# Retention attention and a feed-forward layer in one kernel: second-half queries get a state of their own from unit 6 on, and two of the three attention visits move

## The chip, the cores and the metric

The kernel runs on one core of one Trainium2 chip. The metric is the device time of one execution in microseconds (us). PE is TensorE's matmul side, PEld its weight loads, DVE is VectorE, ACT is ScalarE, POOL is GpSimd, SP is SyncE, which issues most of the DMAs.

## The reference, cut to what matters

Inputs are `q`, `k`, `v` of shape 4 x 8 x 768 x 64 (batch, head, time, width), `w_in` 512 x 2048, `w_out` 2048 x 512 and one `alpha` for each of the 2048 hidden columns.

```python
gamma = 1.0 - 2.0 ** (-5.0 - np.arange(H))
for t in range(S):
    state = gamma * state + k[:, :, t] (outer) v[:, :, t]
    y[:, :, t] = scale * q[:, :, t] @ state
x = y as (B*S, H*D)
h = x @ w_in
out = (np.maximum(h, 0.0) + alpha * np.minimum(h, 0.0)) @ w_out
```

The attention is linear with a decay per head, so it can be done in chunks: inside a chunk by masked scores (q times k, mask, times v), from earlier chunks by a 64 x 64 state per head.

## The kernel before

Time is cut into 12 units of 256 steps, three for each batch element, and each unit into two chunks of 128 (`c` = 0, 1). Two units make a block of 512 rows for the feed-forward layer: six blocks, n = 0 to 5. In each of the later blocks the kernel runs the first matmul stage of block n (`ffn1`: 16 groups of four 128x512 matmuls, L450, each followed by a RELU copy on ACT, L461, and a DVE operation, L463), then the second (`ffn2_seven`), and inside the second it does the attention of the two units of the next block, `u0 = 2 * (n + 1)` and `u0 + 1`.

`ffn2_seven` forms the 512 x 512 result from seven products of 16 matmuls (128x256, L536) instead of eight. They run on two PSUM banks, `ox` (bank 0) and `oy` (bank 1):

- product 1 into `ox`, copied to SBUF by ACT (`kept`, L552, tile `cu`)
- product 2 into a fresh `oy`; DVE adds the copy and stores it (`plus`, L557, tile `os`)
- product 3 added onto `ox`, copied by `kept` (L552)
- product 4 into a fresh `oy`
- product 5 added onto `ox`, using the sum `gs(2)`; copied by `kept` (L552); `plus` (L557) adds `oy` to it
- product 6 added onto `ox`, copied by ACT (L598)
- product 7 added onto `oy`, using `gs(3)`; `plus` (L557)

The sums `gs` of the activations are DVE operations (`g_sums`, L434). The order on every engine is the program's own: `tick(gen, m)` issues the next m matmuls of the products and whatever follows them, and between ticks the attention work is written by hand.

The attention work of a block, as it is before the change, comes in three visits of PE:

- after 8 ticks: `sum_mm` (L249) of both units, the state contribution k times v of each chunk, as 64x64 matmuls, and `score_mm` (L315) of `u0`, two halves of the heads in banks (4, 5) and (6, 7)
- after 48 ticks: `out_mm` of `u0` (state part L364, masked part L382), with its two evictions on ACT (`take_y`, L405, tile `xT`), and `score_mm` of `u0 + 1`
- after 80 ticks: `out_mm` of `u0 + 1` and its evictions

The 256 steps of a unit are kept so that a chunk's 128 keys come as two halves of 64 (`r` = 0, 1). A second-half key touches only second-half queries, so the scores and the masked part use 128 columns for `r` = 0 and 64 for `r` = 1.

The running state goes through `state_sum` and `state_copy`. `state_sum` (L274, L275): DVE adds the contribution in PSUM to the state so far (`ss`), POOL multiplies by the decay (`tf`); the next chunk starts from that. `state_copy` turns `tf` into f16 operands for `out_mm` (tile `th` from unit 6 on): one 64-row half on POOL (L301, `part` 0), the other on ACT (L299, `part` 1). `masks` (L328) are DVE multiplications from PSUM to f16, four for each unit, 384 elements wide.

POOL prepares the next units in `rescale` (L176) and `cast_v` (L192). The first `rescale` of a block waits for `gate`, the last `g_sums` of the block before. SP then transposes (`turn_dma`, L196) and moves the queries (`move_q`, L204); stores and loads share SP's queue. `tab` holds the decay (`dec`), `mj` the mask, `ps(bank, name)` names one of eight PSUM banks.

Of the kernel before, what the change touches and what calls it, by code (L numbers as in the profile page):

```python
# [9 lines left out]
FP = mybir.dt.float32  # L10
F16 = mybir.dt.float16
COPY = mybir.ActivationFunctionType.Copy
SUB = mybir.AluOpType.subtract
RELU = mybir.ActivationFunctionType.Relu
MULT = mybir.AluOpType.mult
ADD = mybir.AluOpType.add
# [5 lines left out]
def kernel(  # L22
# [10 lines left out]
    nc = tc.nc  # L33
# [3 lines left out]
    NP = H // 2  # L37

    SPLIT = 4

    FLIP = 6
    U = 256
    UPB = S // U
# [3 lines left out]
    scale = 1.0 / np.sqrt(D)  # L51
# [9 lines left out]
    for h in range(H):  # L61
        for r in range(2):
            j = 2 * (p_ar % 64) + r
# [10 lines left out]
    sbp = ctx.enter_context(tc.tile_pool(name="sbp", bufs=1, space=bass.MemoryType.SB))  # L74
# [7 lines left out]
    mj = sbp.tile([128, 512], F16, tag="mj", name="mj")[:, 0:384]  # L82
    dec = tab[:, OD : OD + NP].unsqueeze(2).to_broadcast([128, NP, 64])
# [10 lines left out]
    def ps(bank, name, dt=FP, n=512):  # L94
        return psp.tile([128, n], dt, tag=f"b{bank}", name=name)
# [8 lines left out]
    tgbuf = [sbp.tile([128, NP, 128], F16, tag=f"tg{i}", name=f"tg{i}") for i in range(6)]  # L104

    staged, prepped, live, tgs, xT, gts, gsums = {}, {}, {}, {}, {}, {}, {}
    moved = {}
    held, late = [], []

    def behind(ins, other):  # L110
# [20 lines left out]
    def rows(x):  # L131
        return slice(64 * x, 64 * x + 64)

    def load(u, parts="kqv"):
        if u >= NU:
            return
        b, c = divmod(u, UPB)
        t = staged.setdefault(u, {})
        for nm in parts:
            src = {"k": k, "q": q, "v": v}[nm[0]]  # L140
            if nm[0] not in t:
                t[nm[0]] = sbp.tile(
                    [128, H, 2 * D], FP, tag=f"{nm[0]}s", bufs=3, name=f"{nm[0]}s{u}"
                )
            h = slice(0, H) if len(nm) == 1 else slice(4 * int(nm[1]), 4 * int(nm[1]) + 4)
            if u >= SPLIT and nm != "q":
                for x in range(2):
                    for y in range(2):
                        at = U * c + 128 * x + 64 * y
                        nc.sync.dma_start(  # L150
                            out=t[nm][rows(x), :, D * y : D * y + D],
                            in_=src[b, :, at : at + 64, :].rearrange("h p d -> p h d"),
                        )
                continue
            hold(
                nc.sync.dma_start(
                    out=t[nm[0]][:, h, :],
                    in_=src[b, h, U * c : U * c + U, :].rearrange(
                        "h (p r) d -> p h (r d)", r=2
                    ),  # L160
                )
            )
# [70 lines left out]
    def qmove(kq, a, c, p):  # L233
        return kq.rearrange("p (t r a) i -> p t r a i", t=2, r=2)[rows(a), 1, :, p, rows(c)]
# [3 lines left out]
    def sum_mm(u, banks, half=0):  # L238
# [17 lines left out]
        for c in cs:  # L256
            sums[u, c] = sums["t"][c][:, 256 * half : 256 * half + 256].rearrange(
                "p (a e) -> p a e", e=64
            )

    def state(u, c, eng, copy="gg"):

        state_copy(state_sum(u, c, eng), copy)

    def state_sum(u, c, eng):
        if (u, c) not in sums:
            return None
        s = sums.pop((u, c))
        t = sbp.tile([128, NP, 64], FP, tag="tf", bufs=4, name=f"tf{u}_{c}")
        if u % UPB == 0 and c == 0:  # L270
            nc.vector.tensor_tensor(out=t, in0=s, in1=dec, op=MULT)
        else:
            ss = sbp.tile([128, NP, 64], FP, tag="ss", bufs=3, name=f"ss{u}_{c}")
            nc.vector.tensor_tensor(out=ss, in0=run.pop(), in1=s, op=ADD)  # L274
            eng.tensor_tensor(out=t, in0=ss, in1=dec, op=MULT)  # L275
        run[:] = [t]
        return u, c, t

    def state_copy(uct, copy="gg", part=None):

        if uct is None:
            return
        u, c, t = uct
        to = (u, 1) if c == 0 else (u + 1, 0)
        if to[0] >= FLIP:
            tg = tgs.get(to) or tgs.get((to[0], 1 - to[1]))
            if tg is None:
                tg = sbp.tile([128, 2, NP, 64], F16, tag="th", bufs=3, name=f"th{to[0]}")
        else:
            tg = tgbuf[(2 * u + c) % len(tgbuf)]  # L290
        tgs[to] = tg
        for a in range(2):
            far = to[0] >= FLIP and a != to[1]
            if part is not None and far != part:
                continue
            i = t[rows(a)]
            o = tg[rows(to[1]), a] if to[0] >= FLIP else tg[rows(a), :, rows(a)]
            if far or copy[a] == "a":
                nc.scalar.activation(out=o, in_=i, func=COPY, bias=0.0, scale=1.0)  # L299
            else:  # L300
                nc.gpsimd.tensor_copy(out=o, in_=i)  # L301
# [92 lines left out]
    def take_y(u, cs, eng=None):  # L394
        n, ul = divmod(u, 2)
        if n not in xT:
            xT[n] = sbp.tile([128, 2, NP, U], F16, tag="xT", bufs=2, name=f"xT{n}")
        ys = live[u]
        for c in cs:
            o = xT[n][:, ul, :, 128 * c : 128 * c + 128].rearrange("k a (p r) -> k a r p", r=2)  # L400
            i = ys[c].rearrange("k (a r p) -> k a r p", r=2, p=64)
            if eng is not None:
                eng.tensor_copy(out=o, in_=i)
                continue
            nc.scalar.activation(  # L405
                out=o,
                in_=i,
                func=COPY,
                bias=0.0,
                scale=1.0,  # L410
            )
# [11 lines left out]
    def g_sums(n, i, lo, hi):  # L423

        if n not in gsums:
            gsums[n] = sbp.tile([128, 4, HF, U], F16, tag="gt", bufs=2, name=f"gs{n}")
        g = gts[n].rearrange("p (k f) (j t) -> p k f j t", k=2, j=2)
        a11, a12 = g[:, 0, lo:hi, 0, :], g[:, 1, lo:hi, 0, :]
        a21, a22 = g[:, 0, lo:hi, 1, :], g[:, 1, lo:hi, 1, :]
        s1, s2, s3, s4 = (gsums[n][:, x, lo:hi, :] for x in range(4))  # L430
        o, a, b, op = (
            (s1, a21, a22, ADD), (s2, s1, a11, SUB), (s3, a11, a21, SUB), (s4, a12, s2, SUB)
        )[i]
        return nc.vector.tensor_tensor(out=o, in0=a, in1=b, op=op)  # L434
# [177 lines left out]
    def tick(gen, m=10**6):  # L612
        for _ in range(m):
            if next(gen, 1) == 1:
                return
# [171 lines left out]
    for n in range(1, NBLK):  # L787
        more = n + 1 < NBLK
        u0 = 2 * (n + 1)
        if n > 1:  # L790
            gen = ffn1(n, (7, 2, 3, 1, 0, 6, 5, 4, 7, 1, 0, 4, 5, 6, 7, 1))
            if more:
                for u in (u0, u0 + 1):
                    i = rescale(G, u, 0, 0, 8)
                    if u == u0:
                        behind(i, gate)
                    rescale(G, u, 1, 0, 8)
                    turn_dma(u)
                    cast_v(G, u)
                    if u > u0:  # L800
                        load(u + 1, "qv")
                    else:
                        load(u + 2, "k")
                    move_q(u)
                    tick(gen, 8)
            tick(gen)
        gen = ffn2_seven(n, 0, 1) if more else ffn2_seven(n, (0, 3), 1, 2)
        if more:
            tick(gen, 8)
            sum_mm(u0, (2, 3))  # L810
            sum_mm(u0 + 1, (2, 3), half=1)
            score_mm(u0, 0, (4, 5))
            score_mm(u0, 1, (6, 7))
            s00 = state_sum(u0, 0, G)
            state_copy(s00, part=0)
            masks(u0, 0)
            s01 = state_sum(u0, 1, G)
            masks(u0, 1, (0,))
            masks(u0, 1, (1,))
            s10 = state_sum(u0 + 1, 0, G)  # L820
            tick(gen, 8)
            state_copy(s00, part=1)
            state_copy(s01, "aa")
            state_copy(s10, part=0)
            tick(gen, 17)
            state_copy(s10, part=1)
            load(u0 + 3)
            s11 = state_sum(u0 + 1, 1, G)
            state_copy(s11, part=0)
            g_sums(n, 2, 0, HF)  # L830
            tick(gen, 15)
            out_mm(u0, (4, 5))
            score_mm(u0 + 1, 0, (6, 7))
            score_mm(u0 + 1, 1, (2, 3))
            state_copy(s11, part=1)
            masks(u0 + 1, 0)
            masks(u0 + 1, 1)
            gate = g_sums(n, 3, 0, HF)
            tick(gen, 32)
            out_mm(u0 + 1, (4, 5))  # L840
        else:
            tick(gen, 33)
            g_sums(n, 2, 0, HF)
            g_sums(n, 3, 0, HF)
        tick(gen)
# [30 lines left out]
```

## Time and profile before

| what | value |
|---|---|
| median of three runs | 200.97 us (200.62 to 202.11) |
| the profiled execution | 200.52 us, of it span 198.8 us |
| granted TensorE clock, mean | 0.997 |
| L450, first matmul stage | 448 instructions, 349 ns each as modelled |
| L536, seven products | 560 instructions, 273 ns each as modelled |
| L249, state contributions, 64x64 | 320 instructions |
| L315, scores, 64 wide and 128 wide | 384 instructions |
| L364 and L382, attention output from unit 0 on | 80 and 384 instructions |
| L434, activation sums on DVE, 128x2048 | 1.2 us each |
| L275, decay on POOL | 16 instructions, 761 ns each |
| DMA busy share, 98 to 120 us and 152 to 163 us | 0.91 and 0.15 |

A matmul's duration is from its issue to its modelled end, and matmuls overlap; the cost of a row of them is read from the start of the first to the start of what follows. The three blocks that the change touches have their second stage at about 95 to 111, 125 to 140 and 154 to 169 us of the span. The share of PE in the chain that ended last is 79%; DMA's 11% lies in the loads of the first part (keys 4%, `w_in` 4%, `w_out` 4%).

### The profile page before, as it was taken

The numbers are of one execution on the slowest core, as the hardware profiler recorded it, in microseconds if no ns is written. First come the engines' busy times: TensorE is split into PE (matmuls) and PEld (weight loads), VectorE is DVE, ScalarE is ACT, GpSimd is POOL, SyncE is SP. The second block draws the span as 40 slices with busy tenths as digits, with TensorE's granted clock in tenths as the row PEclk, the third lists the DMA queues.
The fourth block names the chain that finished last, engine by engine and source line by source line (L and its number), as shares of the span: only waits on it lengthen the run. The fifth ranks groups of instructions, "written<-read, shape, count | busy, mean of one in ns | idle before, by whom it ended". The sixth has DMA issues, their size and how long they took to land.

```text
span 198.8 us, 5688 instructions
## 1 busy us (share of the span) xinstructions
PE 191.5 (96%) x2365; PEld 127.3 (64%) x2365; DVE 150.6 (76%) x248; ACT 105.7 (53%) x180; POOL 85.5 (43%) x92
## 2 busy tenths in 40 slices
PE   6798999999999999999999999999999999999993
PEld 2466544577477788644788644888544888444882
DVE  7795986527789998389996489993589992689841
ACT  2467675258287435476465466354467365477211
POOL 6288118599439364880065940147910240000000
PEclk9999999999999999999999999999999999999998
DMA  6999999799989989898978998939954011200004
GB/s 170 317 257 132 203 255 248 202 232 214 227 209 176 335 200 241 201 278 189 241 164 199 282 192 182 210 97 231 270 111 93 0 56 56 106 0 3 21 32 158
DMA packets 88184, 34.74 MB, mean 175 GB/s; under 512 B 57936, under 2 KB 87648, under 8 KB 88160
## 3 DMA queue, kind: packets, MB, share of 16 engines
q1 hardware_dynamic: 83760, 30.16, 60.8%
q0 software_dynamic: 4224, 4.19, 13.5%
q8 instruction: 18, 0.29, 0.6%
q10 hardware_dynamic: 176, 0.04, 0.2%
q14 instruction: 6, 0.05, 0.1%
HBM read 27.31 MB, written 6.29 MB: 169 GB/s over the span
## 4 chain that ended last, share of the span: by engine, by line
PE 79%; DMA 11%; DVE 4%; POOL 2%; issue 1%; ACT 1%; POOLq 0%; DVEq 0%
PE hps L450 35%; PE ox L536 16%; PE oy L536 12%; PE ops L488 6%; DMA ks<-in_k_dram 4%; DMA win<-in_moe_w_in_dram 4%; DMA wout<-in_moe_w_out_dram 4%; PE kps L100 2%; PE y L382 2%; PE sca L315 1%; POOL tf L275 1%; PE st L249 1%; DVE m L332 1%; PE y L364 1%; PE oz L536 1%
## 5 line engine op out<-in xcount | busy, mean ns | idle before, releaser
L450 PE MATMUL hps<-xT,win 128*128 128x512 f16 (+1 forms) x448 | 84.7, 349 | 0.7 <-DMA win<-in_moe_w_in_dram 0.7
L463 DVE SCALAR_TENSOR_TENSOR gt<-hm,oma,hps 128x512 f16<-128x512 f32 (+1 forms) x112 | 70.6, 668 | 15.6 <-ACT hm L461 10.7
L461 ACT ACTIVATE hm<-hps 128x512 f32<-128x512 f32 x96 | 57.1, 597 | 31.5 <-PE hps L450 28.6
L450 PEld LDWEIGHTS <-win 128*128 128x128 f16 x448 | 43.5, 98 | 39.3 <-DMA win<-in_moe_w_in_dram 1.2
L536 PEld LDWEIGHTS <-gs 128*128 128x128 f16 x320 | 31.1, 98 | 3.7
L275 POOL TENSOR_TENSOR tf<-ss,tab 128x256 f32<-128x256 f32 x16 | 12.2, 761 | 35.6 <-DVE ss L274 34.7
L176 POOL TENSOR_TENSOR kdq<-ks,tab 128x1024 f16<-128x1024 f32 (+1 forms) x12 | 19.4, 1613 | 16.4 <-DMA ks<-in_k_dram 13.9
L536 PEld LDWEIGHTS <-gt 128*128 128x128 f16 x240 | 22.9, 98 | 4.5
L557 DVE TENSOR_TENSOR os<-oy,cu 128x512 f32<-128x512 f32 x14 | 9.6, 688 | 17.6 <-PE oy L536 13.0
L552 ACT ACTIVATE cu<-ox 128x512 f32<-128x512 f32 (+1 forms) x18 | 9.5, 526 | 24.3 <-PE ox L536 24.3
L176 POOL TENSOR_TENSOR kdq<-qs,tab 128x1024 f16<-128x1024 f32 (+1 forms) x13 | 20.4, 1570 | 3.8 <-DVE wsum L421 3.0
L536 PE MATMUL ox<-wsum,gs 128*128 128x256 f16 x160 | 19.1, 273 | 0.0
L405 ACT ACTIVATE xT<-y 128x512 f16<-128x512 f32 x23 | 15.6, 742 | 4.1 <-PE y L382 3.7
L488 PE MATMUL ops<-wout,gt 128*128 128x512 f16 x64 | 15.3, 380 | 0.1
L192 POOL CAST vx<-vs 128x1024 f16<-128x1024 f32 (+1 forms) x13 | 12.5, 973 | 4.2 <-DMA vs<-in_v_dram 4.2
L434 DVE TENSOR_TENSOR gs<-gt 128x1024 f16<-128x1024 f16 (+1 forms) x14 | 13.0, 932 | 0.3
L225 ACT ACTIVATE kq<-trb 128x1024 f16<-128x1024 f16 x8 | 8.2, 1022 | 7.0 <-PE trb L219 6.9
L536 PE MATMUL ox<-wout,gt 128*128 128x256 f16 x80 | 10.4, 274 | 0.0
L299 ACT ACTIVATE tg<-tf 64x256 f16<-64x256 f32 x11 | 4.5, 414 | 10.2 <-POOL tf L275 5.3
L488 PEld LDWEIGHTS <-gt 128*128 128x128 f16 x64 | 5.8, 98 | 6.2 <-DMA wout<-in_moe_w_out_dram 0.3
L536 PE MATMUL oy<-wsum,gs 128*128 128x256 f16 x80 | 9.6, 273 | 0.1
L536 PE MATMUL ox<-wsum,gt 128*128 128x256 f16 x80 | 9.6, 273 | 0.0
(61 smaller groups left out, 192.3 us busy)
## 6 DMA issues: line engine op xcount, KB each, us to landing
out_dram<-os SPq DMA_DIRECT2D x21, 256.0 KB, 3.1
ks<-in_k_dram SPq DMA_DIRECT2D x32, 128.0 KB, 3.3
qs<-in_q_dram SPq DMA_DIRECT2D x8, 512.0 KB, 5.8
vs<-in_v_dram SPq DMA_DIRECT2D x32, 128.0 KB, 4.8
ks<-in_k_dram SPq DMA_DIRECT2D x8, 256.0 KB, 4.5
qs<-in_q_dram SPq DMA_DIRECT2D x8, 256.0 KB, 4.7
win<-in_moe_w_in_dram POOLq DMA_DIRECT2D x4, 512.0 KB, 8.5
wout<-in_moe_w_out_dram POOLq DMA_DIRECT2D x4, 512.0 KB, 8.0
```

Source lines behind the costliest of these rows:

```text
L176: return eng.tensor_tensor(out=kdq[:, t, :, h0:h1, :].rearrange("p r h d -> p h r d"), in0=staged[u]["kq"[t]][:, h0:h1, :].rearrange("p h ...
L192: eng.tensor_copy(out=o, in_=i)
L275: eng.tensor_tensor(out=t, in0=ss, in1=dec, op=MULT)
L405: nc.scalar.activation(out=o, in_=i, func=COPY, bias=0.0, scale=1.0,)
L434: return nc.vector.tensor_tensor(out=o, in0=a, in1=b, op=op)
L450: nc.tensor.matmul(out=hps[:, f, :].rearrange("p (u t) -> p u t", t=U), lhsT=w_in_all[:, hp, 128 * (f0 + f) : 128 * (f0 + f) + 128], rhs=x ...
L461: nc.scalar.activation(out=hm, in_=hps, func=RELU, bias=0.0, scale=-1.0)
L463: nc.vector.scalar_tensor_tensor(out=gt[:, f0 + f, U * lo : U * hi], in0=hm[:, f, :], scalar=oma_sb[:, f0 + f : f0 + f + 1], in1=hps[:, f, :],
L488: nc.tensor.matmul(out=opss[tq], lhsT=gt[:, ft, 128 * tq : 128 * tq + 128], rhs=w_out_all[:, ft, :], start=(ft == 0), stop=(ft == NFT - 1),)
L536: nc.tensor.matmul(out=o[1][m], lhsT=lhs(f, m), rhs=rhs(f), start=(first and f == 0 and (m == 0 or o[0] is None)), stop=(f == HF - 1), ski ...
L552: nc.scalar.activation(out=to, in_=i, func=COPY, bias=0.0, scale=1.0)
L557: nc.vector.tensor_tensor(out=so, in0=o[0], in1=t, op=ADD)
```

## The change

For units 6 to 11 (blocks n = 2, 3, 4) the loop body is a new one. Blocks before and after keep theirs.

- `halves_mm` replaces `sum_mm`: the contribution of each half chunk goes to its own place in PSUM, so nothing is accumulated; the last unit of a batch element leaves out the half that nobody needs.
- `middle` replaces `state_sum`: DVE first makes the state in the middle of the chunk (`tm`: the state so far plus the first half), then adds the second half (`ss`), then POOL applies the decay (`tf`) as before.
- `middle_copy` turns `tm` into f16, one half on POOL, one on ACT, into tiles `tgbuf` that the earlier units used.
- `half_mm` and `half_masks` replace `score_mm` and `masks`: only the 64x64 scores of keys and queries in the same half chunk are left, so all eight heads fit two banks, and DVE has two masks of 512 elements for a unit instead of four of 384.
- `halves_out` replaces `out_mm`: first-half queries use the state from before the chunk, second-half queries the middle state, and the masked part has 64 columns each. Unit `u0 + 1` has its second chunk evicted by DVE instead of ACT.
- The second visit stands after 64 ticks instead of 48, the third after 96 instead of 80. The copies' and `g_sums`' places move too.
- `tf` has three buffers instead of four, `ss` two instead of three.

In 64x64 matmuls, 32 state products for a unit stay 32 (24 instead of 16 for units 8 and 11), the scores stay 32, the state part of the output goes from 16 to 32 (8 to 24 for units 6 and 9), the masked part stays 32: 112 matmuls more in all.

```diff
+    def halves_mm(u, banks):
...
+        st = [ps(banks[0], "st0"), ps(banks[1], "st1")]
+        for p in range(NP):
+            for r in range(2):
+                for c in range(2):
+                    if last and c == 1 and r == 1:
+                        continue
+                    for a in range(2):
+                        at = 256 * r + 64 * p
+                        nc.tensor.matmul(
+                            out=st[c][rows(a), at : at + 64],
+                            lhsT=kdq[rows(c), 0, r, 2 * p + a, :],
+                            rhs=vx[rows(c), 2 * p + a, r, :],
...
+    def middle(u, c):
...
+        if u % UPB == 0 and c == 0:
+            nc.vector.tensor_copy(out=m, in_=s[:, 0])
+        else:
+            nc.vector.tensor_tensor(out=m, in0=run.pop(), in1=s[:, 0], op=ADD)
+        if u % UPB == UPB - 1 and c == 1:
+            return (u, c, m), None
...
+        nc.vector.tensor_tensor(out=ss, in0=m, in1=s[:, 1], op=ADD)
+        nc.gpsimd.tensor_tensor(out=t, in0=ss, in1=dec, op=MULT)
+        run[:] = [t]
+        return (u, c, m), (u, c, t)
...
+    def halves_out(u, banks, eng=None):
...
+                    h = mids[u] if r else tgs[u, c]
+                    for a in range(2):
+                        q = qmove(kq, a, c, p) if a == c else moved[u][rows(c), :, p, :]
+                        nc.tensor.matmul(
+                            out=at(c, a, p, r),
+                            lhsT=h[rows(c), a, p, :],
+                            rhs=q[:, :, 32 * r : 32 * r + 32],
...
+        take_y(u, (0,))
+        take_y(u, (1,), eng)
...
-        if more:
+        if more and u0 >= FLIP:
+            u1 = u0 + 1
+            tick(gen, 8)
+            halves_mm(u0, (2, 3))
+            halves_mm(u1, (6, 7))
+            half_mm(u0, (4, 5))
+            m00, s00 = middle(u0, 0)
+            half_masks(u0, 0)
+            half_masks(u0, 1)
+            middle_copy(m00, 0)
+            state_copy(s00, part=0)
+            m01, s01 = middle(u0, 1)
+            middle_copy(m01, 0)
+            state_copy(s01, part=0)
+            tick(gen, 8)
+            middle_copy(m00, 1)
+            state_copy(s00, part=1)
+            middle_copy(m01, 1)
+            tick(gen, 17)
+            m10, s10 = middle(u1, 0)
+            middle_copy(m10, 0)
+            state_copy(s10, part=0)
+            load(u0 + 3)
+            g_sums(n, 2, 0, HF)
+            tick(gen, 15)
+            state_copy(s01, part=1)
+            middle_copy(m10, 1)
+            tick(gen, 16)
+            m11, s11 = middle(u1, 1)
+            middle_copy(m11, 0)
+            state_copy(s11, part=0)
+            halves_out(u0, (2, 3))
+            half_mm(u1, (4, 5))
+            state_copy(s10, part=1)
+            middle_copy(m11, 1)
+            half_masks(u1, 0)
+            half_masks(u1, 1)
+            gate = g_sums(n, 3, 0, HF)
+            tick(gen, 16)
+            state_copy(s11, part=1)
+            tick(gen, 16)
+            halves_out(u1, (4, 5), V)
+        elif more:
```

More of the change, by code (lines that the diff above doesn't have):

```diff
@@ L106 @@
     staged, prepped, live, tgs, xT, gts, gsums = {}, {}, {}, {}, {}, {}, {}
-    moved = {}
+    moved, mids = {}, {}
     held, late = [], []
@@ L259, in sum_mm @@
             )
+    def halves_mm(u, banks):
+        kdq, _, vx = prepped[u]
+        last = u % UPB == UPB - 1
+        st = [ps(banks[0], "st0"), ps(banks[1], "st1")]
[10 more added lines that the diff above has]
+                            rhs=vx[rows(c), 2 * p + a, r, :],
+                            start=True,
+                            stop=True,
+                        )
+        for c in range(2):
+            sums[u, c] = st[c].rearrange("p (r a e) -> p r a e", r=2, e=64)
@@ new lines, in middle @@
+    def middle(u, c):
+        s = sums.pop((u, c))
+        m = sbp.tile([128, NP, 64], FP, tag="tm", bufs=2, name=f"tm{u}_{c}")
+        if u % UPB == 0 and c == 0:
[4 more added lines that the diff above has]
+            return (u, c, m), None
+        ss = sbp.tile([128, NP, 64], FP, tag="ss", bufs=2, name=f"ss{u}_{c}")
+        t = sbp.tile([128, NP, 64], FP, tag="tf", bufs=3, name=f"tf{u}_{c}")
+        nc.vector.tensor_tensor(out=ss, in0=m, in1=s[:, 1], op=ADD)
+        nc.gpsimd.tensor_tensor(out=t, in0=ss, in1=dec, op=MULT)
+        run[:] = [t]
+        return (u, c, m), (u, c, t)
@@ new lines, in middle_copy @@
+    def middle_copy(uct, part):
+        u, c, t = uct
+        if u not in mids:
+            mids[u] = tgbuf[u - FLIP].rearrange("p n i -> p (n i)").rearrange(
+                "p (a n e) -> p a n e", a=2, n=NP
+            )
+        for a in range(2):
+            if (a != c) != part:
+                continue
+            if part:
+                nc.scalar.activation(
+                    out=mids[u][rows(c), a], in_=t[rows(a)], func=COPY, bias=0.0, scale=1.0
+                )
+            else:
+                nc.gpsimd.tensor_copy(out=mids[u][rows(c), a], in_=t[rows(a)])
@@ new lines, in half_mm @@
+    def half_mm(u, banks):
+        _, kq, _ = prepped[u]
+        kv = kq.rearrange("p (t r a) i -> p t r a i", t=2, r=2)
+        scs = [ps(banks[0], "sca"), ps(banks[1], "scb")]
+        for p in range(NP):
+            for r in range(2):
+                for c in range(2):
+                    for a in range(2):
+                        at = 128 * p + 64 * r
+                        nc.tensor.matmul(
+                            out=scs[a][rows(c), at : at + 64],
+                            lhsT=kv[rows(a), 0, r, p, rows(c)],
+                            rhs=qmove(kq, a, c, p)[:, :, 32 * r : 32 * r + 32],
+                            start=True,
+                            stop=True,
+                        )
+        live[u] = scs
@@ new lines, in half_masks, with at @@
+    def half_masks(u, a):
+        m2 = sbp.tile([128, 512], F16, tag=f"m2{a}{u % 2}", bufs=2, name=f"m2{a}")
+        nc.vector.tensor_tensor(
+            out=m2.rearrange("p (x i) -> p x i", x=8),
+            in0=live[u][a].rearrange("p (x i) -> p x i", x=8),
+            in1=mj[:, 256:320].unsqueeze(1).to_broadcast([128, 8, 64]),
+            op=MULT,
+        )
+        live[u][a] = m2
+    def halves_out(u, banks, eng=None):
+        _, kq, vx = prepped[u]
+        ys = [ps(banks[0], "y0"), ps(banks[1], "y1")]
+        begun = set()
+        def at(c, a, p, r):
+            return ys[c][rows(a), 128 * p : 128 * p + 128].rearrange(
+                "p (r i) -> p r i", r=2
+            )[:, :, 32 * r : 32 * r + 32]
+        for p in range(NP):
+            for r in range(2):
+                for c in range(2):
+                    if r == 0 and (u, c) not in tgs:
+                        assert u % UPB == 0 and c == 0
+                        continue
+                    h = mids[u] if r else tgs[u, c]
+                    for a in range(2):
+                        q = qmove(kq, a, c, p) if a == c else moved[u][rows(c), :, p, :]
+                        nc.tensor.matmul(
+                            out=at(c, a, p, r),
+                            lhsT=h[rows(c), a, p, :],
+                            rhs=q[:, :, 32 * r : 32 * r + 32],
+                            start=(c, a) not in begun,
+                            stop=False,
+                            skip_group_check=True,
+                        )
+                        begun.add((c, a))
+        for p in range(NP):
+            for r in range(2):
+                for c in range(2):
+                    for a in range(2):
+                        j = 128 * p + 64 * r
+                        nc.tensor.matmul(
+                            out=at(c, a, p, r),
+                            lhsT=vx[rows(c), 2 * p + a, r, :],
+                            rhs=live[u][a][rows(c), j : j + 64],
+                            start=False,
+                            stop=True,
+                            skip_group_check=True,
+                        )
+        live[u] = ys
+        take_y(u, (0,))
+        take_y(u, (1,), eng)
@@ L268, in state_sum @@
         s = sums.pop((u, c))
-        t = sbp.tile([128, NP, 64], FP, tag="tf", bufs=4, name=f"tf{u}_{c}")
+        t = sbp.tile([128, NP, 64], FP, tag="tf", bufs=3, name=f"tf{u}_{c}")
         if u % UPB == 0 and c == 0:
@@ L272, in state_sum @@
         else:
-            ss = sbp.tile([128, NP, 64], FP, tag="ss", bufs=3, name=f"ss{u}_{c}")
+            ss = sbp.tile([128, NP, 64], FP, tag="ss", bufs=2, name=f"ss{u}_{c}")
             nc.vector.tensor_tensor(out=ss, in0=run.pop(), in1=s, op=ADD)
```

## The prediction

> **What bounds the kernel now.** I read the page's header and busy times first, then TensorE's (PE's) order of time through one block of the stretch that changes, then the other engines in the same microseconds.
>
> ```profile
> span 198.8 us, 5688 instructions
> PE 191.5 (96%) x2365; PEld 127.3 (64%) x2365; DVE 150.6 (76%) x248; ACT 105.7 (53%) x180; POOL 85.5 (43%) x92
> ```
>
> PE is busy for 191.5 of 198.8 us. The changed blocks (n = 2, 3, 4) have their second matmul stage from about 95.4 to 111.0, 124.6 to 140.2 and 153.8 to 169.3 us, and there PE has no gap (13.85 us busy in 95.43 to 109.28). So PE's own order decides: what it issues, plus any wait that appears in it. The stage is seven products of 16 matmuls; attention is visited three times between them. I call the point after the k-th yield of the products Tk. Today visit A is at T8, B at T48, C at T80. PE in block n = 2, view in order of time (start, duration, instruction):
>
> ```profile
> 95.64 1.07 PE L536 MATMUL ox<-wout,gt 128*128 128x256 f16 x8
> 96.65 0.71 PE L249 MATMUL st<-vx,kdq 64*64 64x64 f16 x64
> 97.18 0.24 PE L315 MATMUL sca<-kq 64*64 64x128 f16 x1
> ...
> 97.54 0.19 PE L315 MATMUL scb<-kq 64*64 64x64 f16 x1
> 97.67 1.05 PE L536 MATMUL ox<-wout,gt 128*128 128x256 f16 x8
> ```
>
> ```profile
> 98.55 1.91 PE L536 MATMUL oy<-wout,gt 128*128 128x256 f16 x16
> 100.30 1.91 PE L536 MATMUL ox<-wsum,gs 128*128 128x256 f16 x16
> ...
> 103.18 1.92 PE L536 MATMUL oy<-wsum,gs 128*128 128x256 f16 x16
> 104.94 1.91 PE L536 MATMUL ox<-wsum,gs 128*128 128x256 f16 x16
> ...
> 107.03 0.52 PE L382 MATMUL y<-m,vx 64*64 64x128 f16 x32
> 107.53 1.91 PE L536 MATMUL ox<-wsum,gt 128*128 128x256 f16 x16
> 109.28 1.91 PE L536 MATMUL oy<-wout,gs 128*128 128x256 f16 x16
> ```
>
> One product takes 100.30 - 98.55 = 1.75 us from issue to issue (109.4 ns a matmul). So A takes 97.67 - (95.64 + 8 x 0.1094) = 1.15 us, B 103.18 - 102.05 = 1.13, C 107.53 - 106.69 = 0.84. The same reading gives A 1.11, B 1.13, C 0.85 in n = 3 and 1.10, 1.13, 0.84 in n = 4.
>
> The row that matters most is C's end. Products 5 and 6 add up in one bank, `ox`: product 6 (L536, from 107.53) may not write before `kept` (L552) has copied what product 5 left. ScalarE (ACT) and VectorE (DVE) in the same block:
>
> ```profile
> 102.75 0.60 ACT L552 ACTIVATE cu<-ox 128x512 f32<-128x512 f32 x1
> ...
> 106.88 0.60 ACT L552 ACTIVATE cu<-ox 128x512 f32<-128x512 f32 x1 [1.86 <-PE ox L536]
> 107.58 1.35 ACT L405 ACTIVATE xT<-y 128x512 f16<-128x512 f32 x2
> ```
>
> ```profile
> 98.59 0.42 DVE L271 TENSOR_TENSOR tf<-st,tab 128x256 f32<-128x256 f32 x1
> ...
> 101.45 0.68 DVE L557 TENSOR_TENSOR os<-oy,cu 128x512 f32<-128x512 f32 x1
> 102.31 0.42 DVE L274 TENSOR_TENSOR ss<-tf,st 128x256 f32<-128x256 f32 x1 [0.19 <-POOL tf L275]
> 102.65 1.22 DVE L434 TENSOR_TENSOR gs<-gt 128x2048 f16<-128x2048 f16 x1
> ```
>
> The copy ends at 107.48 and product 6 starts 0.05 later; in n = 3 and 4 the copy ends at 136.65 and 165.80, product 6 starts at 136.70 and 165.84. Visit C is as long as that copy: its 0.84 us cost nothing beyond what product 6 would have waited anyhow.
>
> **The change, part by part.**
>
> *Cheaper visits.* Second-half queries get a state of their own, so the 128-column score and output matmuls become 64-column ones. The nearest row for a 64x64 pair (load and matmul, all four quarters of the array in turn) is L249: 64 in 97.18 - 96.65 = 0.53 us, 8.3 ns each. Edges into and out of a visit: 0.13 + 0.12 in A, about 0.19 in B and C. A becomes 64 state + 32 score pairs: 96 x 8.3 ns + 0.25 = 1.05 (units 8 and 11 leave 8 out, but those run on two quarters; taken as equal). B becomes 64 + 32 pairs (56 + 32 for unit 6): 0.80 + 0.19 = 0.99. Gains: A 0.10 + 0.06 + 0.05 = 0.21, B 3 x 0.14 = 0.42. The rate's other end is the score rows, 32 in 97.54 - 97.18 = 0.36 us, 11.3 ns, though half of those have 128 columns; I take 8.3 because its shape is the new one.
>
> *The third visit moves from T80 to T96.* It costs 64 pairs x 8.3 ns + 0.19 = 0.72 there, between products 6 and 7, which use different banks and wait for nothing that it hides: 3 x 0.72 = +2.16. At T80 product 6 now stands right behind product 5, and PE waits for the copy: 0.03 from the last matmul's end (106.85) to the copy's start, 0.60, 0.05, in all 107.53 - 106.69 = 0.84 from issue to issue, exactly what C takes today. So nothing is saved at T80.
>
> *The second visit moves from T48 to T64.* Product 4 starts a fresh `oy`, whose bank DVE's `os` (L557) must have read. B covered that for 1.13 us. Now T48 is 102.05 - 0.10 = 101.95. DVE's list up to `os`, from 98.59: middle (0.42 + 0.03 for a result used at once), sum 0.34 (start to start of a 256-element operation, 98.59 to 98.93), two 512-element masks at 0.60 (L332 rows, 34.91 to 35.52), middle 0.45, sum 0.34: `os` starts at 101.35, ends at 102.03, and PE goes on at 102.09: 0.15 late. In n = 4 (from 156.95, T48 at 160.30) it is also about 0.15; in n = 3 the second sum falls out and `os` is done before T48. Together +0.3; ends 0 and 0.7 (masks at their whole 0.69, twice in each block). The plain copy that replaces the first middle of units 6 and 9 is not in the trace; 0.37 (half of L403's 0.73 for 512 elements) to 0.42.
>
> *What I cost at nothing, and its cover.* DVE in a block: eight masks at 0.465 become four at 0.60 (-1.3 us), four state operations become seven or eight (+1.4), and one eviction of 0.73 (L403) moves from ACT to DVE. `gs2` (L434) comes after `os`, a middle that waits for POOL's `tf`, and a sum: 103.05 to 104.27, needed at product 5, 102.09 + 1.75 + 0.99 = 104.83; 0.56 spare. `gs3`, now queued behind unit u1's masks and so behind visit B's scores, ends near 108.0; product 7 comes at 104.83 + 1.75 + 0.84 + 1.75 + 0.72 = 109.89. POOL's next `rescale` is held behind `gs3` and starts about 1.1 us later (106.94 to 108.1); its six operations then end at 117.5 instead of 116.4, used at 125.8. SP's transpose behind it is today issued at 112.53, when the three stores (110.22 + 2.21) are out, so it moves with the stores and not with POOL. ACT, after the two evictions of B (from 104.4, 1.34), has two far copies (0.42 each) before `kept` is due at 106.74: it comes free at 106.65, so the 0.84 may grow by 0.1 at most by these rows. The last eviction pair has one product (1.75) to hide 0.1 + 0.73. Buffers `tf` 4 to 3 and `ss` 3 to 2: each is read by in-order work long past when it is taken again.
>
> **Sum:** -0.21 - 0.42 + 2.16 + 0.3 = +1.8 us. On the profiled execution's 200.52 (span 198.8 plus 1.7 around it) that is 202.3; that execution lay 0.45 under the median of 200.97, so the forecast is 202.8.
>
> **The rivals.**
>
> 1. *Product 6 hardly waits (faster).* Were the wait at T80 to be w instead of 0.84, a block would change by -0.21 (A and B) + 0.72 + 0.1 - 0.84 + w = w - 0.23; with w = 0 in three blocks -0.7 us, 200.3. It decides at w = 0.23. For it: the list of PE's waits shows none on L552, and C would end at about its time by its own matmuls. Against it: the copy alone is 0.60, it starts only 0.03 after product 5 ends, and three visits with unequal numbers of matmuls all end 0.04 to 0.05 after it.
>
> 2. *The small pairs do not run at 8.3 ns.* If a 64-column pair costs what the mixed score rows cost (11.3 ns), 256 pairs a block are 3.0 ns dearer each: +2.3 us, 205.1. For it: twice as many state products for the same columns, each with its own weight load. Against it: the L249 row has the same shape. The Trainium skill, TensorEngine Tiling (Array Packing), Instruction Overhead, puts about 60 cycles of overhead on each matmul and warns against cutting a dimension that is already small. By it (an estimate from that page: 64 + 60 cycles at 2.4 GHz over four tiles) a pair would take 12.9 ns; the trace's 8.3 ns disagrees, so I keep this rival low.
>
> 3. *The state chain on DVE and POOL is late.* Each middle state waits for POOL's `tf`, which takes 0.61 us alone, but 1.46 (102.88) and 1.44 (131.49) beside DVE's `gs2`. If the first `tf` of a block is stretched so, the second middle, `os` and `gs2` come 0.5 later: +1.0 over n = 2 and 4, 203.8. It decides if a DVE operation with two SBUF operands runs at about 99.6; by the rows the `gs` before it ends at 98.67, so against. The Trainium skill, SBUF — State Buffer, section on its two separate sides, calls the port pair of DVE and GpSimd an exclusive lock, held for the whole instruction; the 1.46 against 0.61 agrees.
>
> **How the numbers follow.** The forecast's case has 0.60; its own range is 201.9 to 203.8 (stall at T48 from 0 to 0.7, edges of the visits, 0.1 at T80). Rival 1 has 0.10, rival 2 0.12, rival 3 0.15; 0.03 is left for a gain that I do not see. One per cent, about what a measurement of this kernel can tell from no change, is 2.0 us, or 202.98: it cuts the forecast's case, 0.35 below and 0.25 above. Slower 0.25 + 0.12 + 0.15 = 0.52; same 0.35 + 0.10 = 0.45; faster 0.03. The range 201.2 to 204.9 leaves out rival 1, the upper half of rival 2, and little else.
>
> **What would show it.** PE idle about 0.7 us before product 6 in each of n = 2, 3, 4, released by ACT `cu`; C of about 0.72 between products 6 and 7; a wait of 0.1 to 0.4 on `os` before product 4 in n = 2 and 4 and none in n = 3; A near 1.05 and B near 0.99. The forecast is wrong if product 6 starts within 0.25 us of product 5's last matmul, if the pairs run at over 10 ns, or if PE waits for `gs2` or a state copy.

## The result and the profile after

The changed kernel takes 203.3 us (median of 22 runs) against 200.66 us for the kernel before in the same comparison: a ratio of 1.0124, 95% interval 1.0099 to 1.0149, so 2.0 to 3.0 us slower. Each ratio here is taken over the executions in the fast state alone, so it is not the quotient of the two medians. The profile's own execution took 203.82 us.

The header and busy times of the page, then the list of PE's waits (who waited for whom; total us, times, longest):

```profile
span 202.1 us, 5942 instructions
PE 191.6 (95%) x2477; PEld 126.7 (63%) x2477; DVE 154.1 (76%) x251; ACT 107.4 (53%) x187; POOL 92.7 (46%) x108
```

```profile
PE ox L670 <- ACT cu L686: 2.1, 3, 0.7
PE hps L584 <- DMA win<-in_moe_w_in_dram: 1.6, 1, 1.6
```

PE is busy as long as before (191.6 against 191.5 us) although it has 112 more matmuls, but a wait has appeared that the list of before did not have: three times 0.7 us, once in each changed block, for the copy `cu` of `kept` (L686 is L552 of before, L670 is L536). (The list also has one new wait of 0.3 us on `trb`, ahead of the changed blocks; the moves alone, below, have it too.) PE in block n = 2, in order of time, with products 3 to 7 and the start of the next first stage:

```profile
101.36 1.91 PE L670 MATMUL ox<-wsum,gs 128*128 128x256 f16 x16
103.22 1.91 PE L670 MATMUL oy<-wsum,gs 128*128 128x256 f16 x16
...
105.99 1.92 PE L670 MATMUL ox<-wsum,gs 128*128 128x256 f16 x16
108.59 1.91 PE L670 MATMUL ox<-wsum,gt 128*128 128x256 f16 x16 [0.69 <-ACT cu L686]
...
111.10 1.92 PE L670 MATMUL oy<-wout,gs 128*128 128x256 f16 x16
112.86 13.98 PE L584 MATMUL hps<-xT,win 128*128 128x512 f16 x64
```

Product 6 starts 2.60 us after product 5, though the 16 matmuls take 1.75: 0.85 us with nothing between them. The third visit now stands between products 6 and 7: 111.10 - (108.59 + 1.75) = 0.76 us. ACT and DVE at the same time:

```profile
107.50 0.40 ACT L314 ACTIVATE tg<-tm 64x256 f16<-64x256 f32 x1
107.95 0.60 ACT L686 ACTIVATE cu<-ox 128x512 f32<-128x512 f32 x1
```

```profile
102.14 0.42 DVE L297 TENSOR_TENSOR ss<-tm,st 128x256 f32<-128x256 f32 x1
102.48 0.68 DVE L691 TENSOR_TENSOR os<-oy,cu 128x512 f32<-128x512 f32 x1
...
104.17 1.22 DVE L568 TENSOR_TENSOR gs<-gt 128x2048 f16<-128x2048 f16 x1
...
107.89 1.22 DVE L568 TENSOR_TENSOR gs<-gt,gs 128x2048 f16<-128x2048 f16 x1
```

The copy starts 0.04 us after product 5's modelled end (105.99 + 1.92), ends at 108.55, and product 6 starts 0.04 later. `os` ends at 103.16 and product 4 starts at 103.22, 0.11 later than product 3 alone would let it.

The second stage, from product 1 to the first matmul of the next first stage, and its parts, in the two profiles (us; a part is its start-to-start time less what the matmuls of the products take, 0.875 for half of product 1 and 1.75 for the others):

| block | stage before | stage after | A before, after | B before, after | C before, after | wait before product 4 | wait before product 6 |
|---|---|---|---|---|---|---|---|
| n = 2 | 15.38 | 16.10 | 1.15, 1.10 | 1.13, 1.02 | 0.84, 0.76 | 0.11 | 0.85 |
| n = 3 | 15.35 | 16.06 | 1.11, 1.15 | 1.13, 1.09 | 0.85, 0.71 | 0.00 | 0.86 |
| n = 4 | 15.34 | 16.06 | 1.10, 1.01 | 1.13, 1.02 | 0.84, 0.72 | 0.19 | 0.86 |
| sum | 46.07 | 48.22 | 3.36, 3.26 | 3.39, 3.13 | 2.53, 2.19 | 0.30 | 2.57 |

The stages are 2.15 us longer. The two profiled spans differ by 3.3 us; 1.12 of that is there when block 2's second stage begins (95.64 before, 96.76 after). The first matmul of the first stage already starts 1.17 us later, at 17.83 instead of 16.66 us; 0.91 of that is a longer wait for the first load of the weights (1.62 instead of 0.71 us), and PE comes to this wait 0.26 later. Whether that belongs to the change is one of the questions below.

### The profile page after: what moved, and what is told of

Read it like the earlier page. It is cut to its first block, busy times and chain, and to the rows that moved or that the text cites. A ratio compares the mean times of both kernels' runs of the same rounds, so it can differ in the third digit from the quotient of the medians.

```text
span 202.1 us, 5942 instructions
## 1 busy us (share of the span) xinstructions
PE 191.6 (95%) x2477; PEld 126.7 (63%) x2477; DVE 154.1 (76%) x251; ACT 107.4 (53%) x187; POOL 92.7 (46%) x108
## 4 chain that ended last, share of the span: by engine, by line
PE 85%; DMA 7%; DVE 2%; ACT 1%; SPq 1%; issue 1%; POOL 1%; POOLq 0%
PE hps L584 41%; PE ox L670 16%; PE oy L670 12%; PE ops L622 7%; DMA win<-in_moe_w_in_dram 4%; DMA vs<-in_v_dram 3%; SPq L158 1%; PE y L516 1%; PE y L369 1%; PE trb L221 1%; PE st L275 1%; ACT cu L686 1%; PE y L383 1%; PE oz L670 1%; PE y L484 1%
## 5 line engine op out<-in xcount | busy, mean ns | idle before, releaser
L670 PEld LDWEIGHTS <-gs 128*128 128x128 f16 x320 | 30.8, 98 | 4.2 <-issue 0.2
L670 PEld LDWEIGHTS <-gt 128*128 128x128 f16 x240 | 23.0, 98 | 7.0 <-issue 2.6
L298 POOL TENSOR_TENSOR tf<-ss,tab 128x256 f32<-128x256 f32 x10 | 8.6, 861 | 38.5 <-DVE ss L297 26.0
L686 ACT ACTIVATE cu<-ox 128x512 f32<-128x512 f32 (+1 forms) x18 | 9.5, 526 | 19.7 <-PE ox L670 19.5
L670 PE MATMUL ox<-wsum,gs 128*128 128x256 f16 x160 | 19.1, 273 | 0.0
L539 ACT ACTIVATE xT<-y 128x512 f16<-128x512 f32 x20 | 13.9, 743 | 8.6 <-PE y L516 4.5
L568 DVE TENSOR_TENSOR gs<-gt 128x1024 f16<-128x1024 f16 (+1 forms) x14 | 12.9, 924 | 0.3
L670 PE MATMUL ox<-wsum,gt 128*128 128x256 f16 x80 | 9.6, 272 | 2.1 <-ACT cu L686 2.1
L409 POOL TENSOR_TENSOR tf<-ss,tab 128x256 f32<-128x256 f32 x8 | 5.7, 709 | 10.4 <-DVE ss L408 10.3
L670 PE MATMUL ox<-wout,gt 128*128 128x256 f16 x80 | 10.4, 274 | 0.0
L670 PE MATMUL oy<-wsum,gs 128*128 128x256 f16 x80 | 9.5, 272 | 0.2
```

The costliest lines, as they stand in the source:

```text
L298: nc.gpsimd.tensor_tensor(out=t, in0=ss, in1=dec, op=MULT)
L670: nc.tensor.matmul(out=o[1][m], lhsT=lhs(f, m), rhs=rhs(f), start=(first and f == 0 and (m == 0 or o[0] is None)), stop=(f == HF - 1), ski ...
L686: nc.scalar.activation(out=to, in_=i, func=COPY, bias=0.0, scale=1.0)
```

## The experiments

Each kernel is compared in the same way: its ratio to the kernel before, and the sum of its three second stages (46.07 before, 48.22 after), which does not contain the start.

### Only the moves: old matmuls, visits at 64 and 96

```diff
-            tick(gen, 15)
+            tick(gen, 15 if u0 < FLIP else 31)
             out_mm(u0, (4, 5))
```

> The kernel before with nothing but the two visits moved (after 64 and 96 ticks instead of 48 and 80, units 6 and up); its matmuls, masks and states are the old ones. Theory (product 6 waits 0.85 us for the copy of product 5 when no visit stands between them): visit B still costs 1.13, visit C its 0.84 at the new place, and the wait of about 0.85 stands where C was: +0.85 in each of three blocks, +2.5 us, about 203.2 against 200.7. Rival 1 (product 6 hardly waits): no more than 0.3 us slower. If instead the new matmuls made the changed kernel slower, this kernel is no slower than before.

Measured: ratio 1.0141, 1.0094 to 1.0187; stages 16.32, 16.15, 16.32, in all 48.79, 2.72 us over before. PE's waits of this kernel, and PE around product 6 of block 2:

```profile
PE ox L536 <- ACT cu L552: 2.1, 3, 0.7
```

```profile
106.06 1.92 PE L536 MATMUL ox<-wsum,gs 128*128 128x256 f16 x16
108.67 1.91 PE L536 MATMUL ox<-wsum,gt 128*128 128x256 f16 x16 [0.69 <-ACT cu L552]
111.20 1.92 PE L536 MATMUL oy<-wout,gs 128*128 128x256 f16 x16
```

The same three waits, with none of the new matmuls, states or masks in the program. The short wait before product 4 is there too: 0.14, 0.00 and 0.18 us. So it is the moves that cost, and the new matmuls give something back: 2.72 against 2.15. It also answers part of the question about the start: this program is the one of before up to block 2, and its stage there begins at 96.64, a microsecond after the 95.64 of before.

### Only the new attention: visits back at 48 and 80

```diff
             tick(gen, 15)
+            halves_out(u0, (2, 3))
+            half_mm(u1, (4, 5))
             state_copy(s01, part=1)
             middle_copy(m10, 1)
-            tick(gen, 16)
             m11, s11 = middle(u1, 1)
             middle_copy(m11, 0)
             state_copy(s11, part=0)
-            halves_out(u0, (2, 3))
-            half_mm(u1, (4, 5))
             state_copy(s10, part=1)
...
             gate = g_sums(n, 3, 0, HF)
-            tick(gen, 16)
+            tick(gen, 32)
+            halves_out(u1, (4, 5), V)
             state_copy(s11, part=1)
-            tick(gen, 16)
-            halves_out(u1, (4, 5), V)
```

> The new matmuls, masks and middle states of the changed kernel with both visits at their old places (48 and 80 ticks). Theory: A and B are 0.06 and 0.11 us shorter in a block and C is hidden, so -0.5 us over three blocks; but the second chunk's middle state reaches its f16 tile about 0.75 us after 48 ticks in blocks 2 and 4, and PE waits there: +1.5. Together about +1.0, 201.7. Rival 2 (64-column pairs are dear): PE's visits themselves take as long as before or longer, without a wait on a copy. Rival 3: more than 1 us of wait in each block, over 203.

Measured: ratio 1.0022, 0.9989 to 1.0055; stages 15.84, 15.26, 15.82, in all 46.92, 0.85 over before. Visit B takes 1.57 us in n = 2 and 1.70 in n = 4, 1.05 in n = 3. PE at the beginning of B in block 2, and POOL there:

```profile
102.16 0.24 PE L369 MATMUL y<-qf,tg 64*64 64x64 f16 x2
102.73 0.21 PE L369 MATMUL y<-kq,tg 64*64 64x64 f16 x1 [0.34 <-POOL tg L318]
```

```profile
101.61 0.61 POOL L298 TENSOR_TENSOR tf<-ss,tab 128x256 f32<-128x256 f32 x1 [0.67 <-DVE ss L297]
...
102.28 0.40 POOL L318 CAST tg<-tm 64x256 f16<-64x256 f32 x1
```

PE stands until the middle state of the second chunk has gone through POOL (102.28 + 0.40, then PE at 102.73). The wait is where it was expected, and smaller than the 0.75 expected: B is 0.44 and 0.57 longer than before, its own saving included. Visit C costs nothing here again, and n = 3, whose second chunk needs no further decay on POOL, gains 0.09. The new attention alone is thus too late for 48 ticks in two blocks of three.

### Third visit back at 80, second left at 64

```diff
             tick(gen, 16)
+            halves_out(u1, (4, 5), V)
             state_copy(s11, part=1)
             tick(gen, 16)
-            halves_out(u1, (4, 5), V)
```

> The changed kernel with its third visit put back after 80 ticks; the second stays at 64. Theory: the visit hides in product 6's wait again, but its last state copies (now ending 0.3 us after product 5) delay it by 0.1 to 0.2: -0.6 us a block against the changed kernel, about 201.5. Rival 1: the visit costs the same wherever it stands, no change, 203.3. Rival 3 (late chain): the masks and copies of the second unit are so late that PE waits over 0.5 us in the visit, and at most half of the 1.8 comes back.

Measured: stages 15.42, 15.29, 15.49, in all 46.20: 2.02 less than the changed kernel and 0.13 over before. PE no longer lists a wait for `cu`. The visit at 80 is 0.95, 0.85 and 1.02 us long, 0.1 to 0.17 over the copy's 0.85 in n = 2 and 4, the size expected for late state copies. In n = 2 the trace agrees: POOL's middle copy ends at 107.89 and PE goes on at 107.90, after a hole in the visit; what lengthens it in n = 4 is not shown. The ratio was 1.0054, 1.0017 to 1.0090, which is 1.1 us, of which the stages explain 0.13. So it was timed and profiled once more:

> The kernel with its third visit at 80 ticks, timed and profiled a second time, since its first ratio (1.0054) said 1.1 us slower than before where its three stages said 0.13. Theory (scatter of the first loads): stages of 15.4, 15.3 and 15.5 again and a ratio between 0.999 and 1.004. Rival: the ratio is over 1.005 again and part of it lies outside the three stages.

Measured: stages 15.43, 15.28, 15.50, in all 46.21; ratio 1.0034, 1.0000 to 1.0067. The stages repeat to 0.01 us each, the ratio is inside the range given, but both ratios lie above what the stages say (1.0006). Three of the eleven executions behind the first ratio had a granted clock of 0.992; by those of 0.997 or more alone the means of the two kernels differ by 0.7 us, and by 0.8 the second time. The half microsecond or so that the stages do not explain stays open. (The second profile had a granted clock of 0.98 before 98 us and the full one in the three stages.)

### The kernel before, a second profile

> The kernel before, profiled a second time. Theory: the first matmul of the first stage waits for the first load of the first weights, and when that load lands differs between executions of one kernel; so this profile's second stage of block 2 may begin anywhere from about 95.4 to 97.1 us (95.64 in the first profile), while its three stages are 15.38, 15.35 and 15.34 us again, to 0.05. Rival: it begins at 95.6 again, and the later beginnings of the other kernels come from their code.

Measured: 200.91 us; stages 15.43, 15.35, 15.33, in all 46.11; block 2's second stage begins at 95.98, the first matmul of the first stage at 17.11 us (16.66 the first time). So that start moves by 0.45 us between two executions of one kernel, while the stages move by 0.04 in sum. Over all profiles whose mean granted clock was 0.997 or more the beginning of block 2's second stage lies between 95.35 and 97.14 us, in no order that goes with the edits: 95.64 and 95.98 before, 96.76 after, 96.64 for the moves alone, 95.64 for the new attention alone, and 97.14 for the fastest kernel of all (below). From the first matmul of the first stage to block 2's second stage these profiles take 78.87 to 78.98 us, but for one with 79.30. So in the profiles the scatter lies ahead of that first matmul, which starts between 16.42 and 18.21 us, long before the changed blocks.

### The copy made twice

```diff
+        if FLIP <= 2 * n + 2 < NU:
+            kept(ox)
         u3 = kept(ox)
```

> The changed kernel with the copy of product 5 made twice by ACT in blocks 2, 3 and 4, one after the other. Theory: product 6 waits for that copy and nothing else, so its distance from the start of product 5 grows by one copy, from 2.60 to about 3.2 us, in each block, +1.9 us in all. Rival 1: the distance grows by less than 0.2 us.

Measured: product 5 to product 6 is 3.09, 3.09 and 3.10 us, against 2.60, 2.61 and 2.61; the stages are 49.75 in all, 1.53 over the changed kernel. ACT and PE in block 2:

```profile
106.66 1.09 ACT L686 ACTIVATE cu<-ox 128x512 f32<-128x512 f32 x2
```

```profile
104.71 1.92 PE L670 MATMUL ox<-wsum,gs 128*128 128x256 f16 x16
107.80 1.91 PE L670 MATMUL ox<-wsum,gt 128*128 128x256 f16 x16 [1.17 <-ACT cu L686]
```

Two copies take 1.09 us from the first start to the last end, not 1.2, so one more copy adds 0.49, and product 6 comes later by that much (the 0.6 expected was one whole copy), 0.05 after the copies' end. So the end of this copy decides when product 6 starts.

### One mask behind the addition

```diff
             half_masks(u0, 0)
-            half_masks(u0, 1)
             middle_copy(m00, 0)
...
             tick(gen, 17)
+            half_masks(u0, 1)
             m10, s10 = middle(u1, 0)
```

> The changed kernel with the same single edit of DVE's order. Theory: the wait before product 4 disappears in blocks 2 and 4 (product 3 to product 4 is 1.75 us from issue to issue instead of 1.86 and 1.94), the wait of 0.85 before product 6 stays; -0.3 us. Rival: the gaps stay, since they are not DVE's.

Measured: product 3 to product 4 is 1.74, 1.75 and 1.74 us; the wait before product 6 stays (2.60, 2.61, 2.60); the stages are 47.78, 0.44 under the changed kernel, of which 0.30 is this wait. Most of the rest is visit A of n = 3, 1.04 instead of 1.15 us, and that is not the edit's: the 32 score pairs there took 0.37 us in the changed kernel's profile, and 0.26 or 0.27 in seven of the eight profiles of its variants, this one among them (0.34 with the visits at 48 and 80). DVE and PE in block 2:

```profile
101.54 0.68 DVE L691 TENSOR_TENSOR os<-oy,cu 128x512 f32<-128x512 f32 x1
102.14 0.68 DVE L341 TENSOR_TENSOR m<-scb,mj 128x512 f16<-128x512 f32 x1
```

```profile
100.80 1.91 PE L670 MATMUL ox<-wsum,gs 128*128 128x256 f16 x16
102.54 1.91 PE L670 MATMUL oy<-wsum,gs 128*128 128x256 f16 x16
```

`os` is done at 102.22, 0.3 before product 4 can start. The short wait was DVE's order, as the prediction had it.

### A bank of its own for product 7

Product 7 goes to bank 6 and runs before product 6; its sum is added to a copy of `oy` plus the second copy of `ox` (`u5`), as the last block of the kernel does already. The cut leaves out lines in `ffn2_seven` by which ACT copies the whole of product 6's bank behind it.

```diff
...
-        gen = ffn2_seven(n, 0, 1) if more else ffn2_seven(n, (0, 3), 1, 2)
+        gen = ffn2_seven(n, 0, 1, 6 if u0 >= FLIP else None, False) if more else ffn2_seven(n, (0, 3), 1, 2)
...
             g_sums(n, 2, 0, HF)
+            gate = g_sums(n, 3, 0, HF)
             tick(gen, 15)
...
-            gate = g_sums(n, 3, 0, HF)
             tick(gen, 16)
             state_copy(s11, part=1)
```

> The changed kernel, visits at 64 and 96, but product 7 gets a bank of its own and runs ahead of product 6, which so no longer stands right behind the copy of product 5 (one more DVE addition in a block; the fourth activation sum is made right after the third). Theory: the three waits of 0.85 us go and nothing takes their place: -2.5 us against the changed kernel, about 200.8, and the three stages are each about 0.15 us shorter than in the kernel before. Rival 1: no change, 203.3. Rival 3: the fourth sum or the added operation is late and PE waits for DVE instead, 0.3 us or more a block.

Measured: stages 15.25, 15.15, 15.23, in all 45.63, 2.59 under the changed kernel and 0.44 under before; ratio 1.0002, 0.9973 to 1.0031. (Its profile had a lower granted clock before 99 us, 0.98, and the full one in the three stages.) No wait for `cu` is left. With the mask behind the addition as well:

> The kernel with a bank of its own for product 7, with one more edit: the second of the two masks of the block's first unit is put behind the addition that frees the bank of product 4. Theory: the waits before product 4 (0.11 and 0.19 us in blocks 2 and 4) go too, so PE waits nowhere in the three stages; they are 15.1 to 15.2 us each instead of 15.35, 0.7 us less than the kernel before over three blocks, about 200.1 against 200.8. Rival: the later mask pushes the third activation sum past the start of product 5 and PE waits there instead, no gain over the kernel without this edit.

Measured: stages 15.23, 15.06, 15.02, in all 45.31, 0.76 under before; ratio 0.9960, 0.9931 to 0.9989. PE and ACT in block 2:

```profile
106.25 1.92 PE L670 MATMUL ox<-wsum,gs 128*128 128x256 f16 x16
108.01 1.91 PE L670 MATMUL oz<-wout,gs 128*128 128x256 f16 x16
...
110.62 1.92 PE L670 MATMUL ox<-wsum,gt 128*128 128x256 f16 x16
```

```profile
108.20 0.41 ACT L314 ACTIVATE tg<-tm 64x256 f16<-64x256 f32 x1 [0.34 <-DVE tm L292]
108.64 0.60 ACT L686 ACTIVATE cu<-ox 128x512 f32<-128x512 f32 x1
```

Product 7 (`oz`) follows product 5 after 1.76 us. The copy even starts later than in the changed kernel, 0.47 after product 5's end, because a middle-state copy stands ahead of it on ACT, and it does not matter: product 6 comes 1.4 us after the copy's end. Timed and profiled again:

> The kernel with a bank of its own for product 7 and the mask behind the addition, timed and profiled a second time: stages of 15.2, 15.1 and 15.0 us and a ratio of 0.996 again, between 0.993 and 0.999. Rival: the gain was the scatter of the first loads, and the ratio is 1.000.

Measured: stages 15.34, 15.07, 15.02, in all 45.43; ratio 0.9975, 0.9939 to 1.0011. The first interval leaves out a ratio of 1, the second does not. The stages say 0.64 to 0.76 us less than before, both times, and that is the firm part: this version beats the changed kernel clearly; that it beats the kernel before, by the stages' 0.3%, the whole times do not show both times.

## Why the prediction was right, point by point

**The third visit and product 6.** Forecast: 0.84 us of wait at product 6 in each block, 0.72 for the visit at its new place, +2.16 in all. Measured: 0.85 to 0.86, and 0.76, 0.71, 0.72, +2.19. Four runs show that it is this mechanism: the moves alone bring the wait with the old matmuls, the third visit back at 80 takes 2.02 away, a second copy lengthens the distance by the copy's 0.49, and a bank of its own takes 2.59 away. Rival 1 is out.

**Product 4 and `os`.** Forecast +0.15, 0 and 0.15. Measured 0.11, 0 and 0.19, and gone when one mask moves behind `os`. The new masks are not needed for it: the moves alone show it as well, with the four old masks ahead of `os`.

**The cheaper visits.** Forecast -0.21 for A and -0.42 for B; measured in this profile -0.10 and -0.26. The first rows of A in blocks 2 and 3:

```profile
97.77 0.74 PE L275 MATMUL st<-vx,kdq 64*64 64x64 f16 x64
98.33 0.21 PE L330 MATMUL sca<-kq 64*64 64x64 f16 x1
```

```profile
127.67 0.69 PE L275 MATMUL st<-vx,kdq 64*64 64x64 f16 x56
128.19 0.21 PE L330 MATMUL scb<-kq 64*64 64x64 f16 x1
```

The 64 state pairs of block 2 take 0.56 us (97.77 to 98.33), 8.75 ns each, not 8.3. For A the forecast was better than this one profile says: in the seven profiles of variants whose 32 score pairs in block 3 take 0.26 or 0.27 us instead of 0.37, A is 3.12 us in sum (3.23 in one), 0.24 less than before. Why these pairs took longer here is not known. B is the term that was mis-sized: 0.99 forecast, and 1.02 at its shortest in any profile with this visit at 64 ticks, which is about what 96 pairs of 8.75 ns and 0.19 of edges give (1.03). In n = 3 it varies from 1.05 to 1.16, and no run tells why. One smaller slip: C of n = 3 has 56 pairs and not 64, since unit 9 is the first of a batch element. Rival 2, 11.3 ns, is out: C's 64 pairs in n = 2 and 4 with 0.19 of edges would take 0.91, and took 0.76 and 0.72. The Trainium skill states about 60 cycles of overhead on each matmul (TensorEngine Tiling (Array Packing), Instruction Overhead), and rival 2's estimate of 12.9 ns a pair adds them to the 64 columns, at a clock of 2.4 GHz that this page does not state. The page's next line, that a free dimension of 1 has the same latency as one of 60, can also be read as a floor, with nothing to add at 64 columns; the measured 8.75 ns a pair speaks against adding.

**What was costed at nothing.** `gs2` ends at 105.39 and product 5 starts at 105.99, 0.60 to spare (forecast 0.56). `gs3` ends at 109.11, product 7 starts at 111.10. POOL's third `tf` in block 2 was stretched to 1.46 beside `gs2`, as in the rows of before, but the first stayed at 0.61, so rival 3 did not come about.

**The sum.** Forecast +1.8 us: 202.8; measured 203.3. That the two are only 0.5 us apart is in part luck: the kernel before came out at 200.66, 0.31 under the 200.97 that the forecast stands on, and the change costs more than forecast. The stages measure +2.15 (-0.10 - 0.26 + 2.19 + 0.30 + 0.04 between old visit C and the wait at product 6 = 2.17), the runs about +2.5 with an interval of 2.0 to 3.0. The stages lie inside it. Of the 0.35 by which the stages exceed the forecast, B is 0.16 and A 0.11, the latter by the slow score pairs of this profile. The further 0.3 of the middle value is not settled. In the eight comparisons that have a ratio, the change of the whole time lies between 0.4 us under and 0.95 us over that of the stages. The start scatters by more than 0.3 us from execution to execution, the moves alone show the later start without any new code ahead of block 2, but no run tells a small shift of the start from that scatter.

## What to carry to other kernels

Work that stands between two matmul groups on the same PSUM bank may be hiding the copy between them; before moving it, look at what starts 0.05 us after a copy ends, even if the list of waits shows nothing. If the work has to move, bring another product into the gap, in a bank of its own, rather than leave the gap open. When an edit sits late in a kernel whose start depends on loads, compare the length of the edited stage as well as the whole time: here it repeated to about 0.1 us in sum where whole spans of one kernel differ by several tenths.

## What the runs showed that was not expected

- Two ACT copies of 128x512 from PSUM in a row take 1.09 us from the first start to the last end, where one takes 0.60: the second adds 0.49, not 0.60.
- The wait of the first matmul of the first stage for its weights differed from 0.58 to 2.10 us between profiles of full granted clock, and the beginning of block 2's second stage from 95.35 to 97.14 us, nearly as much as the whole effect under study.
- A row of small matmuls does not have one price. 32 score pairs of 64 columns took 0.27 us in most profiles and 0.37 in block 3 of the changed kernel's. The 56 state pairs of block 3 took 0.52 us (9.3 ns each) and the 56 of block 4 took 0.45 (8.0 ns each), within 0.01 us in every profile with the new attention, though each block leaves out 8; the cause is open.
